# Packed attention and a gated convolution: q, k and p turned on VectorE in 32x32 blocks, scores in 32x32 array tiles, and three smaller moves

## The chip, the core and the metric

The kernel runs on one core of one Trainium2 chip. The core has a matrix engine (TensorE, PE in the profile), VectorE (DVE), ScalarE (ACT), GpSimd (POOL) and SyncE (SP), which issues the kernel's DMAs. Each works through its own queue in order, and they meet at semaphores. Operands lie in SBUF, 128 partitions wide; TensorE writes to PSUM, which TensorE's results leave through VectorE or ScalarE. The metric is the device time of one launch in microseconds. The profile's span is the part of it from the first to the last instruction of the program.

## The reference, cut to what matters

```python
batch, n_heads, seq, head_dim, n_pack = 8, 8, 576, 64, 32

def sm_attn(qq, kk, vv):
    s = scale * np.matmul(qq, kk.transpose(0, 1, 3, 2))     # scale = 1/8
    s = s - np.max(s, axis=-1, keepdims=True)
    a = np.exp(s)
    a = a / (np.sum(a, axis=-1, keepdims=True) + 1e-09)
    return np.matmul(a, vv)

p_packed = sm_attn(p, k, v)                  # 32 packed rows over 576 tokens
x = sm_attn(q, p_packed, p_packed)           # 576 tokens over 32 packed rows
# heads side by side: x is (8, 576, 512)
gate = sigmoid(causal depthwise convolution of x over the tokens, 5 taps, conv_w)
out = (gate * (x @ w_val)) @ w_out
```

All inputs are fp32 except that the three weights arrive as 64-bit floats, which the kernel takes apart itself.

## The kernel before

Eight batches go through the same chain. In `ORDER` a letter names a stage of a batch, the digit the batch, and `.n` repeats it; each token runs a stage's Python generator to its next `yield`. So the string fixes the order of work on every engine's queue by hand (`InOrder` keeps it), and a token that issues on one engine stands in that engine's queue exactly where the string has it. The stages:

- `K`, `Q`, `V`, `P`, `L` are loads on SP's queue: k, q and v in two pieces a batch (`load`, `load_v`), p for one batch twice over (`load_p`), the weights in nine steps (`load_weights`).
- `W`, `C`, `O` make fp32 weights of the 64-bit words (`from_double`): a scaling on ACT, three bit operations and a product on DVE, then sums on POOL or DVE. `w_out` is split in a high and a low part (`woh`, `wol`).
- `k` and `q` turn k and q so that the head dimension lies on the partitions (`transposed`): six groups of six TensorE transposes a batch for each, of 64x64, through a big PSUM tile and out by an ACT copy that also puts tokens in another order (`(a i b)` and `(i a b)`). `k` starts with `turned`, which does the same for p and scales it.
- `a` (`attn_pack`) is the first attention: `scores`, the maximum on DVE, the exponential with its sum on ACT, transposes of the result in pieces of 96 tokens (`at`, three pairs for each half of the heads), copies, the product with v (`pv`) and the division on ACT (`ppd`). `p` (`packed_turned`) turns the packed rows.
- `s` (`attn_out`) is the second softmax: scores, a turn in 32x32 blocks on DVE out of PSUM, the maximum on DVE, the subtraction on POOL, the exponential on ACT. `t` (`weighted`) sums on DVE, divides on POOL, turns back on DVE, and splits the result into `a2h` and `a2l`.
- `w` (`packed_values`) multiplies the packed rows with `w_val`, so that `v` (`value`) is a product with 32 rows for each head; `v` takes three products of split operands on TensorE, the multiplication with the gate on DVE, the high part on ACT (`gvh`), the low part on DVE (`gvl`).
- `x` (`mixed`) makes x and copies it to `xp`, and `g` (`gate`) convolves it: for each of four column blocks one ACT operation for the first tap, four DVE operations for the others, and a tanh on ACT. Batch 0 (`WHOLE`) goes through `convolved` instead: the packed rows are multiplied with the taps on POOL (`kx`) and TensorE accumulates five shifted products into PSUM; ACT's tanh reads them there, and `g` is empty.
- `o` (`project`) multiplies `gvh` and `gvl` with `woh` and `wol`, 12 products of 512 columns for 128 rows, copies the result and stores it (`put`). The tokens of a batch lie in two planes, even and odd ones, since k and q are read in pairs of tokens (`c=2`), so a store goes out in pieces.

`scores` works with 64 rows of the head dimension by 32 packed rows: eight tiles of the array, four heads by two planes. Products of fp32 operands stand as two records each in the profile.

PSUM has three big tiles of two banks each (`big`), one of one bank (`mid`) and one for `o` (`out`). k, q, scores, x, val and wp all take big tiles. SBUF buffers are counted in `NB`: two for each piece of k, q and v, so that loads run about one batch ahead.

The bar `|` in `ORDER` is where the buffers of the weights' words are given up: `gvh` and `gvl` take their place, so the first `gvh` waits for the last weight. Ahead of the bar stand all of `W`, `C` and `O`, and the loads of the first three to four batches.

Of the kernel before, what the change touches and what calls it, by code (L numbers as in the profile page):

```python
# [26 lines left out]
 'p': 2,  # L27
# [78 lines left out]
def packed_attention_gated_conv(  # L106
# [79 lines left out]
    def load_p(b):  # L186
        t = st["p", b] = tile_of("p", [P, G, 2, D], F32, f"p_{b}")
        for twice in range(2):
            sp.dma_start(t[:, :, twice, :], p[b].rearrange("(g x) j d -> (x j) g d", g=G))
        yield  # L190

    def load(b, nm, src):
        for g in range(G):
            m = st[nm, b, g] = tile_of(f"{nm}m", [P, NB9, 2 * D], F32, f"{nm}m_{b}_{g}")
            sp.dma_start(
                m, src[b, 4 * g : 4 * g + 4].rearrange("h (i n c) d -> (h i) n (c d)", n=NB9, c=2)
            )
            yield
# [17 lines left out]
    def words_of(nm, src, rows):  # L216
        words = tile_of("words", [P, DM, 2], U32, f"{nm}_words", stage)[:rows]
        each = rows // len(src)
        for n, s in enumerate(src):
            sp.dma_start(  # L220
                words[n * each : n * each + each].rearrange("a b c -> a (b c)"), s.bitcast(U32)
            )
# [45 lines left out]
    def paired(x):  # L268

        return x.rearrange("a (j g d) -> a g j d", g=G, d=D)  # L270

    def value_weights(b):
        for c in range(NC):
            words = st["words", "wv"][c]
            yield from from_double(f"wv{c}", words, P)
            pool.tensor_tensor(
                paired(wv[:, c, :]),
                st["top", f"wv{c}"].rearrange("a (g j d) -> a g j d", g=G, d=D),
                words[:, :, 0].bitcast(F32).rearrange("a (g j d) -> a g j d", g=G, d=D),
                op=ALU.add,  # L280
            )
            yield

    def conv_weights(b):
# [3 lines left out]
        taps = words[:, :, 1].bitcast(F32)  # L288
        dve.tensor_tensor(
            paired(taps),  # L290
            top.rearrange("a (g j d) -> a g j d", g=G, d=D),
            words[:, :, 0].bitcast(F32).rearrange("a (g j d) -> a g j d", g=G, d=D),
            op=ALU.add,
        )
# [39 lines left out]
    def transposed(b, nm):  # L334

        for g in range(G):
            m = st[nm, b, g]
            xT = st[f"{nm}T", b, g] = tile_of(f"{nm}T", [P, 4, HS], F32, f"{nm}T_{b}_{g}")
            if nm == "k":
                to = xT.rearrange("x (u j) (a i b) -> x u j i b a", u=2, a=NA, i=32)  # L340
            else:
                to = xT.rearrange("x (u j) (i a b) -> x u j i b a", u=2, a=NA, i=32)
            for part in range(NA):
                pt = big(f"{nm}pt_{b}_{g}_{part}")[:, :, : 64 * NA]
                for n in range(NA):
                    for u in range(2):
                        rows = slice(64 * u, 64 * u + 64)
                        pe.transpose(
                            pt[:, u, 64 * n : 64 * n + 64],
                            m[rows, part * NA + n if nm == "q" else n * NA + part, :],  # L350
                            ident[rows, rows],
                        )
                yield
                act.copy(to[:, :, :, :, :, part], pt.rearrange("x u (n j i) -> x u j i n", n=NA, j=2))
# [391 lines left out]
```

## Time and profile before

| | |
|---|---|
| median of three runs | 309.01 us (308.19 to 310.87) |
| the profiled execution | 306.13 us, of which the span is 304.3 us |
| granted TensorE clock in it | 0.994 of full speed |
| read from HBM, written | 33.57 MB, 9.44 MB |
| DMA packets | 22061, of which 6149 under 512 B |

The page gives an engine's busy time as a union: two operations that overlap in its pipeline count once. Its 40 slices show the same busy shares along the span. A row of a group names the engine, the operation, what is written and read, the shape and the count; behind the bar come the busy time in us and the mean of one operation in ns; behind a second bar the idle time before them and what ended most of it. Nearly all lines are L89, that of `InOrder`, so groups are told apart by their tiles. A row of the chain of waits has a start, a length and what ran.

### The profile page before, as it was taken

What the parts mean: (1) busy time and instruction counts of PE and PEld (TensorE: products, weight loads), DVE (VectorE), ACT (ScalarE), POOL (GpSimd) and SP (SyncE); (2) the same over time, 40 slices, a digit from 0 to 9 for tenths busy, and PEclk for the clock granted to TensorE, in tenths of its full rate; (3) what the DMA queues carried; (4) which work ended last, traced back from release to release, by engine and by line L of the source; (5) the groups of instructions that cost most, each with busy time, mean ns of one, the idle gap of its engine ahead of it and who ended that gap; (6) DMA issues with size and microseconds to landing.
All of it is one profiled execution on the core that took longest, in us unless ns stands there. A gap on an engine that the chain in (4) does not pass through costs nothing.

```text
span 304.3 us, 8095 instructions
## 1 busy us (share of the span) xinstructions
PE 278.2 (91%) x3396; PEld 202.0 (66%) x3396; DVE 249.2 (82%) x388; ACT 207.2 (68%) x421; POOL 58.0 (19%) x62
## 2 busy tenths in 40 slices
PE   1677998968999999999999999999999999999993
PEld 0433555546777677667667767877778776878872
DVE  0465478966989999999899989997999899958761
ACT  2554767847987789778967687768758874565421
POOL 1111352241303120241023101310232003400000
PEclk9999999997999999999999999999999999999999
DMA  7999997281866364674442531445471021211105
GB/s 214 315 234 302 266 235 189 56 241 45 254 198 182 116 155 173 185 218 139 123 149 58 170 111 42 148 112 152 155 216 45 2 69 38 69 71 45 58 0 172
DMA packets 22061, 43.52 MB, mean 143 GB/s; under 512 B 6149, under 2 KB 12293, under 8 KB 22026
## 3 DMA queue, kind: packets, MB, share of 16 engines
q1 hardware_dynamic: 22026, 43.02, 49.5%
q8 instruction: 26, 0.43, 0.6%
q14 instruction: 9, 0.07, 0.1%
HBM read 33.57 MB, written 9.44 MB: 141 GB/s over the span
## 4 chain that ended last, share of the span: by engine, by line
PE 53%; DVE 26%; ACT 10%; issue 4%; DMA 2%; POOL 2%; SPq 2%; ACTq 0%; DVEq 0%; POOLq 0%
PE o L89 20%; DVE sig L89 14%; PE val L89 12%; PE x L89 4%; PE s L89 4%; PE pv L89 3%; PE at L89 3%; DMA wv_words<-in_moe_w_val_dram 2%; DVE mx L89 2%; DVE t L89 2%; ACT sig L89 2%; PE qpt L89 2%; PE kpt L89 2%; SPq L89 2%; DVE gvl L89 2%
## 5 line engine op out<-in xcount | busy, mean ns | idle before, releaser
L89 DVE SCALAR_TENSOR_TENSOR sig<-xp,cw,sig 128x576 f32<-128x576 f32 x112 | 97.4, 870 | 6.5 <-ACT sig L89 5.0
L89 PE MATMUL o<-woh,gvh 128*128 128x512 f32 x144 | 58.9, 409 | 0.8 <-ACT osb L89 0.7
L89 PE MATMUL o<-woh,gvl 128*128 128x512 f32 x144 | 56.4, 392 | 0.0
L89 PE MATMUL o<-wol,gvh 128*128 128x512 f32 x144 | 56.3, 391 | 0.0
L89 PE MATMUL val<-a2h,wph 128*128 128x288 f32 x128 | 40.8, 319 | 4.7 <-ACT qT L89 4.5
L89 POOL TENSOR_TENSOR t<-t,mx 128x576 f32<-128x576 f32 x16 | 23.7, 1481 | 87.8 <-DVE mx L89 87.8
L89 PE MATMUL val<-a2h,wpl 128*128 128x288 f32 x128 | 38.4, 300 | 0.0
L89 PE MATMUL val<-a2l,wph 128*128 128x288 f32 x128 | 38.3, 299 | 0.0
L89 POOL TENSOR_TENSOR t<-t,rs 128x576 f32<-128x576 f32 x16 | 20.6, 1288 | 69.3 <-DVE rs L89 34.0
L89 PEld LDWEIGHTS o<-woh,gvh 128*128 128x128 f32 x144 | 27.0, 188 | 9.1 <-ACT osb L89 2.8
L89 ACT ACTIVATE sig<-sig 128x576 f32<-128x576 f32 x28 | 19.3, 688 | 18.4 <-DVE sig L89 18.2
L89 PEld LDWEIGHTS o<-woh,gvl 128*128 128x128 f32 x144 | 27.0, 188 | 6.2
L89 PEld LDWEIGHTS val<-a2h,wph 128*128 128x128 f32 x128 | 24.6, 192 | 9.4 <-ACT qT L89 4.9
L89 DVE TENSOR_TENSOR gvl<-sig,gvh 128x576 fp32r<-128x576 f32 x32 | 25.0, 783 | 6.6 <-ACT gvh L89 6.6
L89 PEld LDWEIGHTS o<-wol,gvh 128*128 128x128 f32 x144 | 27.1, 188 | 4.7
L89 ACT COPY osb<-o 128x512 f32<-128x512 f32 x34 | 20.0, 589 | 14.1 <-PE o L89 13.7
L89 ACT CAST gvh<-sig 128x576 fp32r<-128x576 f32 x32 | 21.6, 676 | 11.5 <-DVE sig L89 7.4
L89 ACT COPY qT<-qpt 128x384 f32<-128x384 f32 x48 | 26.8, 564 | 3.2 <-PE qpt L89 3.1
L89 DVE SCALAR_TENSOR_TENSOR sig<-sig,val 128x576 f32<-128x576 f32 x32 | 23.7, 742 | 5.5 <-ACT sig L89 3.0
L89 ACT COPY kT<-kpt 128x384 f32<-128x384 f32 x48 | 22.5, 482 | 5.6 <-PE kpt L89 5.1
L89 PEld LDWEIGHTS val<-a2h,wpl 128*128 128x128 f32 x128 | 24.7, 193 | 0.2
L89 PEld LDWEIGHTS val<-a2l,wph 128*128 128x128 f32 x128 | 24.7, 193 | 0.0
(82 smaller groups left out, 474.6 us busy)
## 6 DMA issues: line engine op xcount, KB each, us to landing
km<-in_k_dram SPq DMA_DIRECT2D x16, 576.0 KB, 6.7
qm<-in_q_dram SPq DMA_DIRECT2D x16, 576.0 KB, 4.9
vm<-in_v_dram SPq DMA_DIRECT2D x16, 576.0 KB, 6.0
out_dram<-osb SPq DMA_DIRECT2D x24, 256.0 KB, 2.4
wv_words<-in_moe_w_val_dram SPq DMA_DIRECT2D x8, 256.0 KB, 7.7
wo_words<-in_moe_w_out_dram SPq DMA_DIRECT2D x8, 256.0 KB, 11.0
out_dram<-osb SPq DMA_DIRECT2D x8, 192.0 KB, 2.4
p<-in_p_dram SPq DMA_DIRECT2D x16, 64.0 KB, 6.5
```

Source lines behind the costliest of these rows:

```text
L89: made = getattr(self.engine, op)(*args, **kw)
```

## The change

k and q are loaded so that a partition holds nine neighbouring tokens of each of two heads in a piece; the pieces of a partition are 2304 bytes where they were 4608. `transposed` is two DVE turns of 128x1152 in 32x32 blocks for each of k and q, with no TensorE and no ACT work; p is turned on DVE too, after one ACT scaling for two batches. The head dimension then lies in two halves of 32 (`h`), so `scores` runs in tiles of 32 rows by 32 columns, accumulates over `h`, and writes both halves of the heads (two big tiles) in one call. Tokens come back to natural order where the scores are read (`in_turn`): ACT's exponential and DVE's turn read PSUM in steps of 32 elements. The first attention's transposes take 64 rows instead of 128 and go through one big tile and one copy. `ppd` has a third block and `p` a third transpose. Since tokens are in natural order, `gate` reads plain shifts and `put` is a single store.

Batches 0 to 2 are convolved on TensorE instead of batch 0 alone. `gvl` moves from DVE to POOL for all batches, `a2l` for batches 0 to 2, and one product of the weights' conversion moves from DVE to ACT (a scaling) and POOL (`rest_on_pool`). `ORDER` is another string; its bar stands after 197 tokens of 924, where it stood after 263 of 1195.

```diff
-WHOLE = (0,)
+WHOLE = (0, 1, 2)
...
     def load_p(b):
+        t = tile_of("p", [P, 2, 4, D], F32, f"p_{b}")
+        for e in range(G):
+            for c in range(2):
+                rows = (2 * e + c) * NP
+                of_e = p[b : b + 2].rearrange("b (j e) n d -> e n (b j) d", e=G)[e]
+                sp.dma_start(t[rows : rows + NP].rearrange("a b j d -> a (b j) d"), of_e)
...
+        act.mul(t, t, scale)
...
     def load(b, nm, src):
+        for n in range(2):
+            m = tile_of(f"{nm}m", [P, 2, HS // NP * D], F32, f"{nm}m_{b}_{n}")
+            parts.append(m)
+            at = src[b].rearrange("(j e) (i m) d -> e i j (m d)", e=G, i=2 * NP)
+            sp.dma_start(m, at[:, :, 2 * n : 2 * n + 2])
...
-    def from_double(nm, words, rows, by=1.0, rest_on_pool=False):
+    def from_double(nm, words, rows, by=1.0, rest_on_pool=True):
...
     def transposed(b, nm):
+        for n in range(2):
+            xT = tile_of(f"{nm}T", [P, 2, HS // NP, 2, NP], F32, f"{nm}T_{b}_{n}")
+            parts.append(xT)
+            dve.transpose(
+                xT.rearrange("a j m h i -> a (j m h i)"),
+                st[nm, b][n].rearrange("a j x -> a (j x)"),
+            )
+            yield
...
+    def scores(name, of, xT):
+        two = [big(f"{name}_{e}")[:, :, :HS] for e in range(G)]
+        for h in range(2):
+            for j in range(4):
+                for e in range(G):
+                    for c in range(2):
+                        rows = heads[2 * e + c]
+                        pe.matmul(
+                            two[e][heads[j], c, :],
+                            of(rows, j, h),
+                            xT[j // 2][rows, j % 2, :, h, :],
+                            start=(h == 0),
+                            stop=(h == 1),
+                        )
+        return two
+
+    def in_turn(x):
+        return x.rearrange("a c (m i) -> a c i m", i=NP)
...
     def attn_pack(b):
+            a1t = tile_of("a1t", [TP, 2, NB6, 2 * NP], F32, f"a1t_{b}_{g}")
+            at = big(f"at_{b}_{g}")[:TP, :, : 2 * NB6 * NP]
+            at = at.rearrange("x u (n y) -> x u n y", y=2 * NP)
+            for n in range(NB6):
+                for u in range(2):
+                    rows = slice(64 * u, 64 * u + 64)
+                    pe.transpose(
+                        at[:, u, n], a1s[g][rows, n :: NB6], ident[rows, rows]
+                    )
...
     def attn_out(b):
-            dve.transpose(t2[:, g].rearrange("a (c y) z -> a c (y z)", c=2), s2)
+            dve.transpose(
+                t2[:, g].rearrange("a y z -> a (y z)").rearrange("a (c i m) -> a c i m", c=2, i=NP),
+                in_turn(s2s[g]),
+            )
...
     def weighted(b):
-            dve.tensor_tensor(al[:, gs], a2[:, gs], ah[:, gs].bitcast(F32), op=ALU.subtract)
+            (pool if b < 3 else dve).tensor_tensor(al[:, gs], a2[:, gs], ah[:, gs].bitcast(F32), op=ALU.subtract)
...
     def value(b):
-            dve.tensor_tensor(
+            pool.tensor_tensor(
                 lo, gv, hi.bitcast(F32), op=ALU.subtract
             )
...
     def put(osb, row0, c):
+        sp.dma_start(out_f[row0 + c * P : row0 + c * P + P, :], osb)
```

More of the change, by code (lines that the diff above doesn't have):

```diff
@@ L217, in words_of @@
         words = tile_of("words", [P, DM, 2], U32, f"{nm}_words", stage)[:rows]
[L218 to L222, printed above, removed]
+        sp.dma_start(words.rearrange("a b c -> a (b c)"), src.bitcast(U32))
         return words
@@ L276, in value_weights @@
             pool.tensor_tensor(
[L277 to L280, printed above, removed]
+                wv[:, c, :], st["top", f"wv{c}"], words[:, :, 0].bitcast(F32), op=ALU.add
             )
@@ L287, in conv_weights @@
         top = st["top", "cw"]
[L288 to L294 removed]
+        taps = top
+        dve.tensor_tensor(top, top, words[:, :, 0].bitcast(F32), op=ALU.add)
         yield
@@ L334, in transposed @@
     def transposed(b, nm):
[L336 to L351, printed above, removed]
-                        )
-                yield
-                act.copy(to[:, :, :, :, :, part], pt.rearrange("x u (n j i) -> x u j i n", n=NA, j=2))
-                yield
@@ L357, in scores @@
-    def scores(name, pT, xT, g):
-        s2 = big(name)[:, :, :HS]
-        for j in range(4):
-            for c in range(2):
-                rows = slice(D * c, D * c + D)
-                pe.matmul(s2[heads[j], c, :], pT[rows, g, heads[j]], xT[rows, j, :], start=True, stop=True)
-        return s2
-    def turned(b, nm, x, by):
-        pt = one(f"{nm}t_{b}")
-        for g in range(G):
-            pe.transpose(pt[:, g * P : g * P + P], x[:, g].rearrange("a c d -> a (c d)"), ident)
-        yield
-        xT = st[nm, b] = tile_of(nm, [P, G, P], F32, f"{nm}_{b}")
-        act.mul(xT, pt[:, : G * P].rearrange("a (x y) -> a x y", y=P), by)
-        yield
@@ L375, in keys @@
-    def keys(b):
-        yield from turned(b, "pT", st["p", b], scale)
+        parts = st[f"{nm}T", b] = []
+        for n in range(2):
+            xT = tile_of(f"{nm}T", [P, 2, HS // NP, 2, NP], F32, f"{nm}T_{b}_{n}")
[4 more added lines that the diff above has]
+            )
+            yield
+    def scores(name, of, xT):
[11 more added lines that the diff above has]
+                            stop=(h == 1),
+                        )
+        return two
@@ L429, in packed_turned @@
     def packed_turned(b):
-        yield from turned(b, "ppT", st["ppd", b], 1.0)
+        pt = one(f"ppTt_{b}")
+        for n in range(3):
+            pe.transpose(pt[:, n * P : n * P + P], st["ppd", b][:, n], ident)
+        yield
+        ppT = st["ppT", b] = tile_of("ppT", [P, 3, P], F32, f"ppT_{b}")
+        act.copy(ppT, pt[:, : 3 * P].rearrange("a (n x) -> a n x", n=3))
+        yield
     def attn_out(b):
@@ L434, in attn_out @@
         mx = tile_of("mx2", [P, G, NBLK], F32, f"mx2_{b}")
+        s2s = scores(
+            f"s2_{b}", lambda rows, j, h: st["ppT", b][rows, h, heads[j]], st["qT", b]
+        )
+        yield
         for g in range(G):
-            s2 = scores(f"s2_{b}_{g}", st["ppT", b], st["qT", b, g], g)
-            yield
-            dve.transpose(t2[:, g].rearrange("a (c y) z -> a c (y z)", c=2), s2)
+            dve.transpose(
+                t2[:, g].rearrange("a y z -> a (y z)").rearrange("a (c i m) -> a c i m", c=2, i=NP),
+                in_turn(s2s[g]),
+            )
             yield
@@ L489, in packed_values @@
                 rows = slice(D * g, D * g + D)
-                pe.matmul(wp[heads[j], g, :], ppT[rows, g, heads[j]], wv[rows, j, :], start=True, stop=True)
+                pe.matmul(wp[heads[j], g, :], ppT[rows, 2, heads[j]], wv[rows, j, :], start=True, stop=True)
         yield
@@ L524, in mixed @@
             for n in range(2):
-                act.copy(xps[n][:, :, half, PAD:], two[n][:, :, :HS])
+                act.copy(xps[n][:, :, PAD + half * HS : PAD + half * HS + HS], two[n][:, :, :HS])
                 yield
     def convolved(b):
-        kx = tile_of("xp", [P, 2, 2, PAD + HS], F32, f"kx_{b}")
-        kx = kx.rearrange("a n c m -> a (n c m)")[:, : G * NT * D]
+        kx = tile_of("xp", [P, 2, PAD + S], F32, f"kx_{b}")
+        kx = kx.rearrange("a n m -> a (n m)")[:, : G * NT * D]
         kx = kx.rearrange("a (g k d) -> a g k d", g=G, k=NT)
@@ L547, in convolved @@
             for back in range(NT):
-                src = (half + back) % 2
-                skip = (back + src - half) // 2
+                skip = back if half == 0 else 0
+                end = half * HS + HS - back
                 for g in range(G):
```

190 lines of the change are left out of this document (80 added, 110 removed).

## The prediction

> **What bounds the kernel now.** I read the page's engine totals first, then its 40 slices, then the stages.
>
> ```profile
> span 304.3 us, 8095 instructions
> PE 278.2 (91%) x3396; PEld 202.0 (66%) x3396; DVE 249.2 (82%) x388; ACT 207.2 (68%) x421; POOL 58.0 (19%) x62
> PE   1677998968999999999999999999999999999993
> DVE  0465478966989999999899989997999899958761
> DMA  7999997281866364674442531445471021211105
> GB/s 214 315 234 302 266 235 189 56 241 45 254 198 182 116 155 173 185 218 139 123 149 58 170 111 42 148 112 152 155 216 45 2 69 38 69 71 45 58 0 172
> ```
>
> The shares alone make PE and DVE rivals; the slices part them. PE stands at 9 from slice 11 to the end, while DVE is low in the first eight slices and again in the last five. The table by stage (engine busy time, clock, DMA share, GB/s) puts numbers to it. It is cut at 66 us, about where the order's bar lies (stage buffers given up for gvh and gvl), and at 80 and 260:
>
> ```profile
> core 0: us, PE busy (x) PEld busy (x) DVE busy (x) ACT busy (x) POOL busy (x), PEclk, DMA share, GB/s
> 0.00:66.00 66.00, 50.40 (x850) 29.22 (x850) 40.97 (x76) 39.68 (x92) 16.73 (x20) 1.00 0.88 230
> 66.00:80.00 14.00, 10.24 (x160) 8.15 (x158) 8.98 (x16) 9.75 (x21) 5.32 (x6) 0.88 0.51 137
> 80.00:260.00 180.00, 178.26 (x2174) 132.66 (x2174) 170.35 (x259) 138.62 (x279) 33.77 (x34) 1.00 0.44 130
> 260.00:304.00 44.00, 39.35 (x220) 31.99 (x218) 28.88 (x40) 19.17 (x31) 2.22 (x4) 1.00 0.20 69
> ```
>
> Three stages follow. Up to 66 us neither engine is full and the DMA share is 0.88: loads and dependencies set the pace. From 80 to 260 us PE is idle for 1.7 us and DVE for 9.7: PE is the bound, DVE close behind. At the end PE works alone. Behind 66 us PE has 278.2 - 50.4 = 227.8 us of work in 238.3 us, so 10.5 us of idling. The chain's last pieces show the tail:
>
> ```profile
> PE 53%; DVE 26%; ACT 10%; issue 4%; DMA 2%; POOL 2%; SPq 2%; ACTq 0%; DVEq 0%; POOLq 0%
> 294.96 0.76 DVE L89 TENSOR_TENSOR gvl<-sig,gvh 128x576 fp32r<-128x576 f32 x1 [0.74 <-ACT gvh L89]
> 290.85 5.50 PE o L89 x24
> 297.01 3.03 PE o L89 x12
> ```
>
> DVE's last gvl ends at 295.7, the last product at 300.0; the 4.3 us behind it are the copy and the store.
>
> **What goes away, and its price.**
>
> ```profile
> L89 PE MATMUL kpt<-ident,km 64*128 64x64 f32 x288 | 19.6, 260 | 3.2 <-DMA km<-in_k_dram 2.8 <-ACT sig L89 0.2
> L89 PE MATMUL qpt<-ident,qm 64*128 64x64 f32 x288 | 18.8, 246 | 0.3 <-ACT sig L89 0.2
> L89 PE MATMUL pTt<-ident,p 128*128 128x128 f32 x16 | 4.1, 348 | 6.1 <-DMA p<-in_p_dram 6.1
> L89 PE MATMUL at<-ident,a 128*96 128x128 f32 x96 | 21.8, 312 | 2.9 <-ACT a1t L89 2.5 <-ACT pT L89 0.2
> L89 ACT COPY qT<-qpt 128x384 f32<-128x384 f32 x48 | 26.8, 564 | 3.2 <-PE qpt L89 3.1
> L89 ACT COPY kT<-kpt 128x384 f32<-128x384 f32 x48 | 22.5, 482 | 5.6 <-PE kpt L89 5.1
> L89 DVE SCALAR_TENSOR_TENSOR sig<-xp,cw,sig 128x576 f32<-128x576 f32 x112 | 97.4, 870 | 6.5 <-ACT sig L89 5.0
> L89 DVE TENSOR_TENSOR gvl<-sig,gvh 128x576 fp32r<-128x576 f32 x32 | 25.0, 783 | 6.6 <-ACT gvh L89 6.6
> L89 DVE TENSOR_TENSOR a2l<-a,a2h 128x576 fp32r<-128x576 f32 x16 | 12.2, 763 | 1.1 <-ACT a2h L89 1.1
> L89 DVE SCALAR_TENSOR_TENSOR wo_words<-wo_words 128x512 f32<-128x512 uint32 x4 | 2.8, 690 | 0.1
> ```
>
> PE loses the turns of k, q and p: 19.6 + 18.8 + 4.1 = 42.5 us. ACT loses 49.3 us of copies; it was at 207 and is nowhere the bound, so that alone buys nothing. DVE loses the gates of batches 1 and 2, 32 x 0.870 = 27.8; gvl, 25.0; six a2l, 4.6; eight products of the weights' halves, 8 x 0.69 = 5.5. Together 62.9 us.
>
> **What comes in.** The nearest rows:
>
> ```profile
> L89 DVE STREAM_TRANSPOSE a<-t 128x576 f32<-128x576 f32 x16 | 12.3, 768 | 0.1
> L89 DVE TENSOR_TENSOR sm<-sm,eps 128x18 f32<-128x18 f32 x16 | 2.8, 178 | 0.5
> 7.48 1.23 PE L89 MATMUL kpt<-ident,km 64*128 64x64 f32 x18 [0.68 <-DMA km<-in_k_dram]
> 48.92 2.65 PE x L89 x80
> 112.06 0.67 PE x L89 x16
> 75.00 0.65 PE s L89 x16
> 73.85 0.81 PE pv L89 x48
> L89 PE MATMUL ppTt<-ident,ppd 128*128 128x128 f32 x16 | 3.4, 297 | 0.5 <-ACT ppd L89 0.5
> L89 POOL TENSOR_TENSOR wv<-wv_top,wv_words 128x512 f32<-128x512 f32 x4 | 5.1, 1284 | 18.9 <-DVE wv_words L89 18.9
> ```
>
> DVE gets 32 turns of 128x1152. No row has that size. Two of 576 stand for one at most, 1.54 us. The tiny operation of 18 elements takes 0.178 us, so (0.768 - 0.178)/558 is 1.06 ns for each further element, and 1152 come to 1.37 us; were the fixed part 0.3, it would be 1.24. I take 1.37, so 43.8 us (40 to 49). Eight turns of 128x256 for p come to 0.43 each in the same way, 3.4 us. DVE: 249.2 - 62.9 + 43.8 + 3.4 = 233.5, before contention. Its turns and maxima of the scores read PSUM in strides of 32 now; the trace has no such read on DVE, and a few tenths on 32 operations would be up to 10 us, in the range.
>
> PE's new scores: a set was two calls of 16 records on eight array tiles, two records to a tile, 0.65 us a call, 1.3 us a set. Now it is one call of 64 records on sixteen tiles, four records to a tile: twice the 0.65, again 1.3 us. The x rows bear that out: ten records to a tile take 2.65 us, two take 0.67, so 0.25 us for each further one. Change: nothing. By the x rows a set could take 0.67 + 2 x 0.25 = 1.17, -2 us in all; were records issued one by one at the s row's 0.65/16 = 0.04 us, a set would take 2.6 us, +21 us; the pv row (48 records in 0.81 us, 0.017 each) speaks for the low end.
>
> The trace's 0.017 us per record can be set against the Trainium skill, TensorE: Matmul & The Clock Gate, "Wait — 56ns, not 53.3ns?", which says that matmuls never start closer than about 25 ns however small. By that rule a set of 64 would need 1.6 us and the 16 sets 4.8 us more, 291 us for the whole. The pv row disagrees with the floor.
>
> The at turns become 192 of half the rows; 18 of that kind took 1.23 us, 0.068 each, 13.1 us for 21.8 (with strided weights, unknown here, at most the old 21.8). A third ppT turn adds 1.7. Convolving batches 1 and 2 on PE adds four halves of 2.65 - 0.67, 7.9 us. PE: 278.2 - 42.5 - 8.7 + 1.7 + 7.9 = 237 us (235 to 267).
>
> POOL gets 32 gvl and 6 a2l at 1.284 x 576/512 = 1.44 (54.7 us), nine weight products at 1.28 (11.5) and two kx: 58 becomes some 128 of 280. Its queue is in order, so the subtraction and division of the second softmax now stand behind gvl, and ACT's exp and DVE's turn of a2 behind those; one such wait is 1.44 us and is covered as long as DVE has other work, which at 80 to 260 it has. In the tail the last gvl costs 1.44 - 0.78 = +0.7 us on the path.
>
> SP has fewer stores (36 for 48) and the same bytes; p comes for two batches at once in four loads, ahead of the bar twice, and its one buffer holds SP's queue only until the second batch's turn, which stands some fifty tokens ahead of the next load. Loads ahead of the bar come to 15.4 MB in either order, counted from the tokens, which at the 230 GB/s of the first stage is 66 us again. The k and q rows come in pieces half as long, so I see no faster head.
>
> **The sum.** I counted both orders' tokens with these durations. Before: 278.7 us of PE, 42.7 ahead of the bar; the page has 278.2. (For DVE the count is 258 where the page has 249, since its operations overlap a little.) After: 237 of PE, 26 ahead of the bar and 211 behind; DVE has 49 ahead of it, where it had 44. So much of PE's relief lies in the head, where it isn't worth anything, and what counts is the stage behind the bar: 236 becomes 211. The measured head held 7.7 us more PE work than the count (50.4 against 42.7: PE runs ahead of the bar, and lone calls are longer), so 211 - 6 = 205 remain at 66 us. Span: 66 + 205 + 10.5 idle = 282. DVE's own sum: 233.5 + 7 of contention (below) + 25 idle in the head (66 - 41) + 9 behind its last work = 274; it is just below, so PE stays the bound by a little. The profiled execution took 306.1 us for its span of 304.3, and the median is 309.0, 0.9% more: 282 + 1.8 = 284, put to the median 286.
>
> **The rivals.**
>
> ```profile
> L89 DVE SCALAR_TENSOR_TENSOR sig<-xp,cw,sig 128x576 f32<-128x576 f32 x17 | 13.9, 817 | 2.9 <-ACT sig L89 2.5
> 130.79 2.69 DVE L89 SCALAR_TENSOR_TENSOR sig<-xp,cw,sig 128x576 f32<-128x576 f32 x2
> 131.19 1.67 POOL L89 TENSOR_TENSOR t<-t,mx 128x576 f32<-128x576 f32 x1
> L89 DVE SCALAR_TENSOR_TENSOR sig<-sig,val 128x576 f32<-128x576 f32 x32 | 23.7, 742 | 5.5 <-ACT sig L89 3.0
> ```
>
> Slower: GpSimd and VectorE block each other. The first row is the gate in the last 40 us, where POOL does nothing: 0.817 against 0.870 over all. Beside the POOL operation at 131.19, two gates took 2.69 us, 1.05 more than 2 x 0.82. So a POOL operation costs DVE (0.870 - 0.817) x 112 = 5.9 us over the 41 tensor operations of POOL (32 of the second softmax, eight of the weights, kx), 0.14 on average, and 1.05 at worst. The 49 new ones cost 7 to 51 us. I take 7: the average is over operations placed as these are, among mixed DVE work, and turns and reductions, which take one operand, make up more of DVE now. It decides from (304.3 - 34 - 233.5)/49 = 0.75 us each; at 1.05 the span is 233.5 + 51 + 34 = 319, some 324 us as a median. The Trainium skill, SBUF — State Buffer, "Who interferes with whom", says that a DVE instruction with two SBUF inputs and a GpSimd instruction that reads SBUF exclude each other for a whole instruction; the pair at 130.79 agrees with it, and so does the other multiply-add, whose second input is in PSUM and which stays at 0.742.
>
> Little gain: scores now hold two of the three big PSUM tiles until DVE and ACT have read them. If PE stood for a reduction and an exp, 1.5 us, in each of 16 sets, that is 24 us and a span of 306; half of it 294, a median of 298. For it: val also frees its tile only through DVE. Against it: 25 big tiles a batch become 15, and PE went 180 us with 1.7 of idling.
>
> More gain: the head isn't bound by its loads. At the 261 GB/s that its first six slices average the 15.4 MB take 59 us, at 302 only 51, so the bar could lie some 10 us earlier, and the span end near 272, 276 as a median; with DVE's floor of 274 for the span it hardly goes further than 270.
>
> That PE's removed work was hidden anyway is a rival only for the head, and there it is already counted as worth nothing.
>
> **How the numbers follow.** Forecast (PE bound behind the bar, 276 to 296): 0.70. More gain, 276 or less: 0.08. Little gain, 296 to 306: 0.11. Port contention decides, 306 and up to 324: 0.11. The range 270 to 303 leaves out the contention case and a sliver of the others. A measurement of this kernel tells 1% from no change (its three runs span 0.9%), so faster is below 306: 0.82, with a part of the little-gain case at no change, 0.07, and slower 0.11.
>
> **What would show it.** Right: no kpt and qpt rows; PE near 237 busy; DVE near 240, with 32 turns of 1.3 to 1.4 us; the gate's mean below 0.95; PE at 9 from the bar to the end. Wrong: a gate's mean of 1.2 or more with DVE at 270 (contention); s calls of 2 us or more (issue of small tiles); PE idle for tens of us between 80 and 260 us, released by DVE (PSUM tiles); the first gvh well away from 66 us (the head).

## The result, and the profile after

| | before | after |
|---|---|---|
| median | 309.94 us (308.19 to 310.88) | 301.01 us (298.55 to 301.14) |
| ratio, 95% interval | | 0.970 (0.963 to 0.977) |
| the profiled execution's span | 304.3 us | 299.2 us |

The changed kernel is 3.0% faster. The forecast was 286 us, 7.5% less; 301 lies near the upper end of the range of 270 to 303. The first fence is the page of the changed kernel: the span, the engines' totals, and the slices of PE and of its granted clock.

```profile
span 299.2 us, 8542 instructions
PE 259.6 (87%) x3676; PEld 192.0 (64%) x3676; DVE 245.2 (82%) x349; ACT 164.4 (55%) x306; POOL 124.6 (42%) x107
PE   0465555989999998999999999999999979999984
PEclk9998555899999999999999999999999979999998
```

PE's busy time fell by 278.2 - 259.6 = 18.6 us, ACT's by 42.8, DVE's by 4.0, and the span by 5.1. So PE's idle time grew by 13.5, from 26.1 to 39.6. The table by stage says where (busy time of PE, PEld, DVE, ACT and POOL, then clock, DMA share and GB/s, as in the table of before):

```profile
0.00:66.00 66.00, 37.15 (x838) 22.51 (x838) 46.70 (x75) 32.74 (x65) 28.66 (x30) 0.79 0.87 238
66.00:80.00 14.00, 12.95 (x257) 9.82 (x244) 13.55 (x23) 8.47 (x15) 13.92 (x11) 1.00 0.63 183
80.00:260.00 180.00, 175.91 (x2417) 133.10 (x2423) 163.14 (x230) 107.16 (x201) 73.84 (x63) 0.99 0.41 126
260.00:299.20 39.20, 33.63 (x188) 26.54 (x172) 21.80 (x24) 16.05 (x26) 8.14 (x6) 0.98 0.18 68
```

Ahead of 66 us PE does 13.3 us less and the time stays: as forecast, that part buys nothing. The first gvh starts at 68.9 us, where it started at 68.6 (rows of gvh, with the first and the last start):

```profile
L82 ACT CAST gvh<-sig x32: 658/675/687, 68.9 to 288.8; 128x576 fp32r<-128x576 f32 x32
```

Behind 66 us PE is idle for 1.05 + 4.1 + 5.6 = 10.7 us, about the 10.5 forecast, but has 222.5 us of work where 205 were forecast. DVE, whose idle time was 55.1 us of the span before, has 54.0 now: hardly less. The groups of the changed kernel (busy, mean ns, idle before them):

```profile
L82 DVE SCALAR_TENSOR_TENSOR sig<-xp,cw,sig 128x576 f32<-128x576 f32 x80 | 76.5, 957 | 8.7 <-ACT sig L82 7.2
L82 POOL TENSOR_TENSOR gvl<-sig,gvh 128x576 fp32r<-128x576 f32 x32 | 48.4, 1514 | 79.7 <-ACT gvh L82 79.7
L82 DVE STREAM_TRANSPOSE qT<-qm 128x1152 f32<-128x1152 f32 x16 | 21.6, 1358 | 0.0
L82 DVE STREAM_TRANSPOSE kT<-km 128x1152 f32<-128x1152 f32 x16 | 21.5, 1350 | 2.6 <-DMA km<-in_k_dram 2.5
L82 DVE STREAM_TRANSPOSE pT<-p 128x256 f32<-128x256 f32 x8 | 3.4, 429 | 0.9 <-ACT p L82 0.9
L82 PE MATMUL at<-ident,a 64*96 64x64 f32 x192 | 13.4, 281 | 1.8 <-ACT a L82 1.8
```

The turns cost what they were put at, and so do the at turns. The gate does not: 957 ns, where 870 was the mean before and 950 was named as the bound of being right. The chain of waits shows the tail, which PE ended alone before. Now DVE's gates of batch 7 stand on it from 270 us on (some of its pieces: start, length, what ran):

```profile
271.62 2.08 DVE sig L82
273.72 0.83 DVE sig L82
277.67 2.08 DVE sig L82
284.58 1.86 DVE sig L82
```

A gate takes 0.83 us, or 2.08 where GpSimd's subtraction runs beside it, as this row of the timeline has it for the first:

```profile
271.64 1.43 POOL L82 TENSOR_TENSOR gvl<-sig,gvh 128x576 fp32r<-128x576 f32 x1 [8.55 <-ACT gvh L82]
```

### The profile page after: what moved, and what is told of

It reads as the page before. It is cut to its first block, busy times and chain, and to the rows that moved or that the text cites. A ratio compares the mean times of both kernels' runs of the same rounds, so it can differ in the third digit from the quotient of the medians.

```text
span 299.2 us, 8542 instructions
## 1 busy us (share of the span) xinstructions
PE 259.6 (87%) x3676; PEld 192.0 (64%) x3676; DVE 245.2 (82%) x349; ACT 164.4 (55%) x306; POOL 124.6 (42%) x107
## 4 chain that ended last, share of the span: by engine, by line
PE 56%; DVE 23%; DMA 9%; ACT 5%; issue 3%; SPq 2%; POOL 1%; POOLq 1%; ACTq 0%; DVEq 0%
PE o L82 23%; DVE sig L82 13%; PE val L82 11%; PE x L82 8%; PE s L82 5%; DMA vm<-in_v_dram 3%; PE pv L82 3%; DMA wo_words<-in_moe_w_out_dram 3%; PE at L82 3%; DMA km<-in_k_dram 2%; DVE sm L82 2%; DVE kT L82 2%; SPq L82 2%; PE wp L82 1%; ACT sig L82 1%
## 5 line engine op out<-in xcount | busy, mean ns | idle before, releaser
L82 DVE SCALAR_TENSOR_TENSOR sig<-xp,cw,sig 128x576 f32<-128x576 f32 x80 | 76.5, 957 | 8.7 <-ACT sig L82 7.2
L82 POOL TENSOR_TENSOR gvl<-sig,gvh 128x576 fp32r<-128x576 f32 x32 | 48.4, 1514 | 79.7 <-ACT gvh L82 79.7
L82 PE MATMUL o<-woh,gvl 128*128 128x512 f32 x144 | 57.3, 398 | 1.0 <-POOL gvl L82 1.0
L82 PE MATMUL o<-wol,gvh 128*128 128x512 f32 x144 | 56.9, 395 | 0.0
L82 PE MATMUL val<-a2h,wph 128*128 128x288 f32 x128 | 39.6, 310 | 0.0
L82 PE MATMUL val<-a2h,wpl 128*128 128x288 f32 x128 | 37.8, 295 | 0.0
L82 DVE SCALAR_TENSOR_TENSOR sig<-sig,val 128x576 f32<-128x576 f32 x32 | 23.7, 740 | 9.9 <-PE val L82 5.6
L82 POOL TENSOR_TENSOR t<-t,mx 128x576 f32<-128x576 f32 x16 | 20.8, 1299 | 19.5 <-DVE mx L82 19.4
L82 PE MATMUL pv<-vm,a1t 96*32 96x64 f32 x768 | 16.7, 239 | 13.9 <-ACT a1t L82 8.0
L82 PEld LDWEIGHTS pv<-vm,a1t 96*32 96x32 f32 x768 | 13.4, 121 | 22.5 <-ACT a1t L82 14.4
L82 PE MATMUL s<-kT,pT 32*32 32x288 f32 x512 | 17.2, 479 | 12.1 <-DVE kT L82 11.7
L82 ACT CAST gvh<-sig 128x576 fp32r<-128x576 f32 x32 | 21.5, 673 | 10.5 <-DVE sig L82 9.4
```

The lines of the kernel that those rows point to most:

```text
L82: made = getattr(self.engine, op)(*args, **kw)
```

## The experiments

Each ran beside the kernel before on the same chip; a ratio is to that one. Where one leaves work out, its expectation says which.

**Is TensorE the only bound of the kernel before?** Its turns twice (the pair of `pe.transpose` in `transposed`):

```diff
+                        for again in range(2):
                             pe.transpose(pt[:, u, 64 * n : 64 * n + 64], ...)
```

> The kernel before with each TensorE turn of k and q issued twice. It measures what one of the 576 turns costs on the path. PE theory: the 348 behind 79 us add 0.048 us each, 17 us, those ahead of it little: 322 to 332 us against 309. At the price that the prediction used, 0.068 us for all 576, it would be 348. If the turns only fill gaps of PE: 309 to 314.

Measured: 317.79 us, ratio 1.034 (1.027 to 1.041), some 10 us for 576 further records: less than the PE theory's 322, more than the 314 of records that only fill gaps. Without q's turns and copies, and without those of both k and q (a constant tile takes the place of the result):

```diff
+        for g in range(G):
+            st[f"{nm}T", b, g] = any_x
...
+        return
```

> The kernel before without the turns of q: 288 TensorE turns and 48 ScalarE copies are left out, and a constant stands in q's place in the second softmax (q is still loaded). It measures what half of the removed work was worth. The prediction's price, 18.8 us by the group row or 0.068 us each: 290 us or less against 309. Stream theory (behind 79 us q's turns hold PE for 9.9 us, in the head they are worth nothing): 297 to 301. If they only fill gaps: 306 to 309.

> The kernel before without the turns of k and of q: all 576 TensorE turns and their 96 ScalarE copies are left out, and a constant stands for both (k and q are still loaded). It is what taking this work from TensorE can give at best in that order of work. The prediction's terms (38 us of PE, 25 of it behind the bar): 284 us or less against 309. Stream theory, from q alone (ratio 0.980): twice that, 295 to 300.

Measured: 303.67 us, 0.980 (0.973 to 0.988), and 307.06 us, 0.994 (0.988 to 0.999); neither lies in a range that was named for it. The page of the one without either, totals and chain of waits:

```profile
span 304.5 us, 6816 instructions
PE 256.7 (84%) x2820; PEld 181.1 (59%) x2820; DVE 249.3 (82%) x388; ACT 166.8 (55%) x325; POOL 59.2 (19%) x63
DVE 37%; PE 30%; DMA 18%; ACT 6%; issue 4%; POOL 2%; SPq 2%; ACTq 0%; POOLq 0%; DVEq 0%
```

The same kernel in the table by stage:

```profile
80.00:260.00 180.00, 166.50 (x1818) 122.16 (x1810) 169.68 (x257) 114.04 (x219) 33.91 (x34) 0.97 0.40 118
```

21.5 us of PE's busy time and 40 of ACT's are gone, and the span is that of before. From 80 to 260 us PE is 11.8 us less busy and DVE as busy as before (169.68 for 170.35): DVE's 10 us of idling there are no slack that it can give up. Now the other side, DVE relieved and PE not, by leaving gvl out (the third product takes gvh), and both:

```diff
-            dve.tensor_tensor(lo, gv, hi.bitcast(F32), op=ALU.subtract)
...
-        for n, (w, x) in enumerate(((gvh, woh), (gvh, wol), (gvl, woh))):
+        for n, (w, x) in enumerate(((gvh, woh), (gvh, wol), (gvh, woh))):
```

> The kernel before without gvl: VectorE's 32 subtractions (25 us) are left out, and the third product takes gvh in gvl's place, so PE does the same work. Leaving PE's turns out was worth 2 us. One-bound theory for VectorE (PE's relief is worth nothing because VectorE alone sets the pace): 25 us less, 284 to 290. Two-bound theory (PE and VectorE stand at the same height, either one alone holds the time): 300 to 307.

> The kernel before without gvl (as in the other run) and without the TensorE turns and copies of k and q (a constant stands for them). Two-bound theory: both engines are relieved, so more than the two single reliefs together: 280 to 290. If the pace is set by neither but by the chain of waits of a batch: 300 or more.

Measured: without gvl 305.65 us, 0.992 (0.987 to 0.998); without both 299.51 us, 0.968 (0.958 to 0.978). The page's chain of the one without gvl:

```profile
PE 73%; DVE 9%; ACT 7%; DMA 4%; issue 4%; POOL 2%; SPq 0%; ACTq 0%; POOLq 0%; DVEq 0%
```

and in the table by stage:

```profile
80.00:260.00 180.00, 179.45 (x2213) 134.46 (x2209) 156.94 (x240) 141.56 (x284) 34.44 (x35) 1.00 0.46 134
```

Either relief alone is worth under 1%, both together 3.2%. TensorE and VectorE were two bounds of about the same height. With both relieved the two-bound theory had 280 to 290, though; 299.51 is far above that, so something else stands close behind them, and no run here says what. That q's turns alone gave 2%, more than k's and q's together, shows how far a fixed order adds or takes a few us of its own: differences of 1% between such kernels settle nothing.

**What bounds the changed kernel?** The same there: without the third product (gvl is still computed), without DVE's turns of k and q, and without both:

```diff
-        for n, (w, x) in enumerate(((gvh, woh), (gvh, wol), (gvl, woh))):
+        for n, (w, x) in enumerate(((gvh, woh), (gvh, wol))):
```

> The changed kernel without the third product of the projection (gvl with woh: 144 of 432 records, 33 us of PE); gvl itself is still computed. If PE's sum alone sets the pace behind the bar: 268 to 273 us against 301. If VectorE follows close behind (245 us busy, and 34 idle at both ends): 279 to 288. If VectorE and the waits between queues set it: 290 or more.

> The changed kernel without VectorE's 32 turns of k and q (43 us of VectorE; a constant stands for k and q, which are still loaded). If only PE's sum sets the pace behind the bar: 295 to 302 us against 301, the gain being the head's. If VectorE's queue is on the path beside PE's (putting 24 us of gvl back on it and taking 15 us of waiting off cost 8): 285 us or less.

> The changed kernel without VectorE's turns of k and q (43 us of VectorE, a constant stands for them) and without the third product (33 us of PE). Each alone gave 298 and 296 against 301. Two-bound theory: both bounds fall, 265 to 275. If something else (loads, GpSimd, the chain of waits) stands at the same height: 290 or more.

Measured: 296.19 us, 0.954 (0.946 to 0.962); 298.39 us, 0.961 (0.953 to 0.969); 290.33 us, 0.941 (0.932 to 0.950). The changed kernel stands at 0.970, so the reliefs of 22.5 us on PE, of some 43 on DVE, and of both bring about 5, 3 and 9 us. The last was put at 265 to 275 by the two-bound theory and missed that, as its counterpart in the kernel before did. The page of the first, with its chain:

```profile
span 294.8 us, 8250 instructions
PE 237.1 (80%) x3532; PEld 169.6 (58%) x3532; DVE 247.7 (84%) x349; ACT 164.1 (56%) x306; POOL 125.6 (43%) x107
DVE 49%; PE 28%; ACT 8%; DMA 6%; issue 4%; POOL 2%; SPq 1%; DVEq 0%; ACTq 0%; POOLq 0%
```

This kernel has the 237 us of PE that the prediction counted, and ends at 295 with DVE as half of its chain, not at 282. Last, gvl left out, the subtraction on GpSimd with it (the third product takes gvh):

```diff
-            pool.tensor_tensor(lo, gv, hi.bitcast(F32), op=ALU.subtract)
```

> The changed kernel without gvl: GpSimd's 32 subtractions are left out, the third product takes gvh. VectorE is no longer held up by them (the gate's mean of 0.957 us should fall to 0.85, 9 us in all), PE's work is the same. Two-bound theory: 296 to 301, as VectorE's relief by 43 us gave 298. Blocking theory (GpSimd's hold on VectorE is what eats the gain): 290 or less.

Measured: 291.26 us, 0.943 (0.936 to 0.950). Its page, with the chain and the gate's row:

```profile
span 289.9 us, 8511 instructions
PE 256.7 (89%) x3676; PEld 190.9 (66%) x3676; DVE 231.7 (80%) x349; ACT 164.2 (57%) x306; POOL 77.0 (27%) x75
PE 80%; DMA 6%; DVE 4%; issue 3%; ACT 3%; SPq 1%; POOL 1%; DVEq 0%; ACTq 0%; POOLq 0%
L82 DVE SCALAR_TENSOR_TENSOR sig<-xp,cw,sig 128x576 f32<-128x576 f32 x80 | 66.1, 826 | 10.2 <-ACT sig L82 8.9
```

The same kernel in the table by stage:

```profile
0.00:66.00 66.00, 38.43 (x848) 23.21 (x850) 46.88 (x76) 32.86 (x65) 29.72 (x30) 1.00 0.87 238
80.00:260.00 180.00, 179.83 (x2467) 136.23 (x2466) 156.10 (x231) 110.55 (x206) 37.68 (x38) 1.00 0.42 128
```

32 subtractions on another engine are gone, TensorE's work is the same, and the span falls by 9.3 us. TensorE is busy for 179.83 of 180 us and is 80% of the chain: 290 is its own bound in this order. DVE lost 245.2 - 231.7 = 13.5 us without having lost an instruction, 10.4 of it on the gates.

Both kernels issue their products in the same order (the third with gvh in gvl's place), so their traces can be laid side by side: TensorE in the changed kernel is 1.4 us behind the other at 78 us, 4.3 at 229, 7.8 at 247 and 9.3 at the end. The largest step stands in the changed kernel's chain, and behind it the same twelve products without gvl:

```profile
234.83 1.50 DVE sig L82 x2
236.35 2.08 DVE sig L82
238.46 1.61 DVE sig L82
241.53 0.58 ACT osb L82
242.16 4.61 PE o L82 x12
```

```profile
235.96 3.06 PE o L82 x12
```

Two gates take 2.08 and 1.61 us for 0.83, ScalarE's tanh waits for the last gate, the copy of osb stands behind that tanh in ScalarE's queue, and TensorE waits 2.1 us for the copy. Its granted clock is then 0.57 from 242.2 to 246.2 us, and twelve products take 4.61 us. So VectorE's delay reaches TensorE through ScalarE's queue; for gvl itself TensorE waits only 1.0 us in all, by its row of o<-woh,gvl.

**Is it GpSimd's hold on VectorE?** The hold is the time by which a VectorE operation is longer because one of GpSimd runs beside it. The subtraction twice, the second time into a tile that is read no more:

```diff
             pool.tensor_tensor(lo, gv, hi.bitcast(F32), op=ALU.subtract)
+            pool.tensor_tensor(gv, gv, hi.bitcast(F32), op=ALU.subtract)
```

> The changed kernel with each gvl subtraction on GpSimd issued twice, the second into a tile that nobody reads any more, so that gvl itself is no later than before and only GpSimd's traffic doubles. Theory that this traffic holds VectorE back and that this is the 10 us between the changed kernel and the one without gvl: 308 to 312 us, and a mean gate above 1050 ns (957 with one, 826 with none). If the 10 us are the waits of TensorE for gvl and not VectorE's hold: 301 to 304 us, gate below 1000 ns.

Measured: 319.31 us, 1.041 (1.031 to 1.050). Page, chain and gate:

```profile
span 316.1 us, 8567 instructions
PE 266.3 (84%) x3676; PEld 194.5 (62%) x3676; DVE 259.0 (82%) x349; ACT 164.6 (52%) x306; POOL 178.4 (56%) x139
DVE 41%; PE 29%; POOL 12%; ACT 6%; DMA 5%; issue 4%; SPq 1%; DVEq 0%; ACTq 0%; POOLq 0%
L82 DVE SCALAR_TENSOR_TENSOR sig<-xp,cw,sig 128x576 f32<-128x576 f32 x80 | 87.5, 1094 | 9.6 <-ACT sig L82 8.4
```

With 0, 32 and 64 subtractions on GpSimd DVE is busy for 231.7, 245.2 and 259.0 us: 0.42 and 0.43 us for each. The gate takes 826, 957 and 1094 ns; 2, 12 and 24 of the 80 gates take more than 1.2 us. That is the blocking theory's result for the gate; the span grew by 16.9 us, more than its 7 to 11. GpSimd itself is 12% of this chain, where it was 1% of the changed kernel's: the next gvl can stand behind the added operation in its queue, and this run doesn't separate that part from the hold. The Trainium skill, SBUF — State Buffer, "Who interferes with whom", has a VectorE instruction with two SBUF inputs contend for a shared port pair with a GpSimd instruction that reads SBUF; the 2.08 us gates and this row of three agree. Moving the subtraction alone, back to DVE in the changed kernel and to GpSimd in the kernel before:

```diff
-            pool.tensor_tensor(
+            dve.tensor_tensor(
                 lo, gv, hi.bitcast(F32), op=ALU.subtract
```

> The changed kernel with gvl back on VectorE, all else kept. PE theory (behind the bar PE is the bound in both kernels; the change took little PE work away there, because the turns of k and q cost only some 0.048 us each when they run in a stream, and convolving two more batches and 1.6 us for a score set ate most of that): PE's work is the same, so 296 to 304 us against 301. VectorE's busy time goes from 245 to about 254 (32 x 0.75 = 24 us come in, some 15 us of waiting for GpSimd go). Blocking theory (PE only looks busy, GpSimd's gvl holds VectorE's gate operations up, and that sets the pace): 290 us or less.

> The kernel before with gvl on GpSimd instead of VectorE, nothing else. PE theory: VectorE's sum falls by about 25 - 15 us, PE's stays, so 305 to 310. If VectorE's queue is on the path as much as PE's (putting gvl back cost the changed kernel 8 us): 299 to 304. If GpSimd's holding up of gate operations weighs more where there are 112 of them: 312 or more.

Measured: 308.72 us, 1.001 (0.996 to 1.005), and 321.74 us (315.97 to 323.32) against 311.33, whose runs scatter too much for a ratio. The first lies outside what both theories had, 296 to 304 and 290 or less. So in the new order the place on GpSimd is worth 8 us in spite of the hold (DVE is at 257.8 busy with gvl, 245.2 without it), and in the old order it costs 5 by its fastest run and 10 by its median. Each order was written for its own placement; a single move out of it is no clean measure.

**What do the small scores cost?** All of `scores` twice, and a second pass over a third of the columns:

```diff
+        for again in range(2):
             for h in range(2):
...
-                            two[e][heads[j], c, :],
+                            two[e][heads[j], c, : HS // (1 + 2 * again)],
```

> The changed kernel with the products of every score set issued twice (the second pass starts anew, the result is the same). PE theory: 16 sets x 1.55 us = 25 us more PE work, of which the four sets in the head count little: 318 to 327 us. Blocking theory: PE has room, so 301 to 309 us.

> The changed kernel with a second pass over every score set on only 96 of the 288 columns (the same values are written again). The full second pass cost 25.5 us, 0.025 us for each of 1024 records. If a record of the 32x32 tiles costs its issue, whatever its length: the third costs as much, 322 to 328 us. If it costs its columns: 8 to 9 us, so 309 to 311.

Measured: 326.49 us, 1.061 (1.053 to 1.068), and 318.69 us, 1.028 (1.020 to 1.037). The first fence has two sets in the changed kernel's chain, one in the head and one behind the bar; the others have a set in the chain of the kernel with two passes and of the one with a pass and a third:

```profile
30.31 2.51 PE s L82 x63
97.59 1.53 PE s L82 x63
```

```profile
112.94 2.90 PE s L82 x125
```

```profile
108.18 2.26 PE s L82 x85
```

Taken from the first to the last record, a set takes 1.60 us, 2.97 twice, and 2.33 with the third: 1.37 for a full pass of 64 records and 0.73 for a short one. So a full set costs more than the 1.3 us forecast, but the ten sets behind 79 us occupy 16.6 us in the changed kernel, 3.6 more than at 1.3 each, and not twice as much, as single issue would have it. In the times, 16 further passes cost 25 to 28 us, more than their 22, and 16 short ones 18, more than their 12; the 318.69 lies between what was put for a price by issue and by columns.

**Which batches belong on TensorE?** Batch 1 convolved on it in the kernel before; batch 7 too in the changed one; batch 7 in place of batch 2 there; and a product of `ident` that nobody reads issued before every second token ahead of the bar, to keep TensorE's clock up in the head:

```diff
-WHOLE = (0,)
+WHOLE = (0, 1)
...
-WHOLE = (0, 1, 2)
+WHOLE = (0, 1, 2, 7)
...
-WHOLE = (0, 1, 2)
+WHOLE = (0, 1, 7)
...
+            if fill and at % fill == fill - 1:
+                pe.matmul(idle[:, :P], ident, ident, start=True, stop=True)
```

> The kernel before with batch 1 convolved on PE as well (its gate tokens dropped, the rest of x's tokens of batch 1 set behind the last of v's of batch 0). PE gets 2 x 2.4 = 4.8 us, VectorE loses 16 gate operations, 13 to 14 us. PE theory: 311 to 315. If VectorE's relief counts for as much as PE's burden: 304 to 309.

> The changed kernel with batch 7 convolved on PE as well (its gate stage is empty), order otherwise the same. PE gets 2 x 2.4 = 4.8 us more, VectorE loses 16 gate operations, which from 264 us on stand in the chain at 6.05 us for each of the four column blocks. PE theory in its strict form (only PE's sum counts): 303 to 306 us. Tail theory (the last 25 us of the changed kernel are a chain of gate operations that GpSimd's gvl holds up, 2.08 us for 0.83): 290 to 297 us.

> The changed kernel with batches 0, 1 and 7 convolved on TensorE in place of 0, 1 and 2: batch 2 goes through the gate on VectorE, batch 7 doesn't, so VectorE has as many gates as before and TensorE as many products, but 13 us of gate work lie between 80 and 140 us, where VectorE is busy for 15 to 17 of each 20 us, and no longer near the end. Theory that two bounds of about the same height hold the span, VectorE's (with GpSimd's hold) late and TensorE's (290) all through: 295 to 298 us. If TensorE alone sets the end, no gain: 300 to 302. If the order by hand fits only its own placement: 301 to 306.

> The changed kernel with a fill-in product of 128x128 (its result is read by nobody) behind every second entry of the order ahead of the bar. PE's granted clock is at half in the records from 27.6 to 54.9 us, and score sets there take 2.6 us for 1.53. If the cold clock in the head is on the path: 293 to 298 us against 301. If the head is set by loads and VectorE: 300 to 302. If the fill-ins stand in the way of the chain of the first batches: 304 or more.

Measured: 313.87 us, 1.014 (1.006 to 1.022); 304.13 us, 0.989 (0.982 to 0.996); 318.07 us, 1.034 (1.028 to 1.040); and 309.79 us against 308.88, from four runs of which one took 301.55, two 309.8 and one 1387 us, so that no ratio is given and the clock's part stays open. None beats the changed kernel. Batch 7 on TensorE came out where the strict PE theory had it, at 303 to 306. The third was to take 13 us of gates from the tail; its stages from 120 to 140 and from 280 us on:

```profile
120.00:140.00 20.00, 11.03 (x116) 7.22 (x116) 16.38 (x24) 10.64 (x21) 1.16 (x1) 0.75 0.21 60
280.00:318.00 38.00, 32.96 (x231) 26.83 (x230) 4.40 (x6) 7.84 (x16) 5.71 (x4) 1.00 0.17 63
```

The longest of PE's waits about there (what waited for what: us, times, longest):

```profile
PE at L85 <- DVE sig L85: 4.4, 1, 4.4
PE x L85 <- ACT a L85: 3.7, 2, 3.0
```

DVE is indeed done early, with 4.4 us of work in the last 38, but PE idles for 9 us from 120 to 140, half of it behind a gate, and ends alone and late. It missed by 20 us what it was put at, and says only that the order must move with the work; whether gates placed earlier can pay stays open.

## Why the prediction came out as it did

**Right.** The direction; the head (first gvh at 68.9 us, 66 forecast, and TensorE's 13.3 us of relief ahead of it worth nothing); the turns (1.35 for 1.37 us, 0.43 for 0.43); the at turns (13.4 for 13.1 us); POOL's sum (124.6 for 128); the little-gain rival set aside, since PE is idle for 4 us from 80 to 260 and not for tens.

**The step that failed first: DVE's floor.** The prediction had DVE's "own sum: 233.5 + 7 of contention (below) + 25 idle in the head (66 - 41) + 9 behind its last work = 274". The idle time in it was too small. It was 55 us in the profile before, and the step kept 34 of it, as if the 21 us between were PE's doing and would go with PE's load. Most of them stay when PE is relieved: 55.2 without the turns (304.5 - 249.3), 54.0 in the changed kernel, 47.1 where PE has 237 us of work. The waits of DVE in the kernel before, from 80 us on (us, times, longest), name ACT first, not PE:

```profile
DVE sig L89 <- ACT sig L89: 8.1, 8, 2.5
DVE gvl L89 <- ACT gvh L89: 3.6, 5, 0.7
```

With 47 to 55 of idling the floor comes to 233.5 + 7 + 47 to 55 = 288 to 296 before any other error: above the 282 given as PE's bound. So the step "PE stays the bound by a little" fails, and the run with 237 us of PE, which ends at 294.8, shows it. Such a floor is no law: without gvl DVE idles for 58.2 us, because there PE sets the pace.

**The hold.** "a POOL operation costs DVE ... 0.14 on average": 32 gvl alone cost 13.5 us, 0.42 each, where 7 were put for all 49. This is the rival of port contention, right in its mechanism, at a price between its ends (0.14 and 1.05) and short of the 0.75 from which it would have made the kernel slower. That gvl meets gates, with their two operands in SBUF, more often than the second softmax's operations did would explain it; no run separates that. Without gvl the span is 9.3 us shorter: more than half of the 17.2 between the span of 299.2 and the 282 forecast. Taking some 43 us of turns off VectorE brought only 3 us, so these 9 aren't VectorE's sum; the traces point to where the held gates stand, ahead of osb at 242 us and in the tail.

**TensorE's sum.** "205 remain at 66 us" were 218.3 in the kernel without gvl, where PE is busy nearly throughout (256.7 less the 38.43 ahead of 66 us), and that one ended at 289.9. These 13.3 us more of work, less 5 us of idling that went (10.5 forecast, 5.6 there), are the other 8 us of the miss. PE's work behind 66 us fell by 227.8 - 218.3 = 9.5 us, where 227.8 - 205 = 22.8 were counted. Taken from the start of a block of products to that of the next, behind 79 us, and that kernel set against the one before: k's and q's turns had occupied 16.8 us for 348 records, 0.048 each, where 0.068 came from a lone group and would make 23.7; the at turns gave back 1 us, where 8.7 were counted for the whole kernel from rows whose records overlap their neighbours'; x took 8.4 us more (7.9 forecast for all four halves); ten score sets took 15.3 us, 2.3 more than at 1.3 each.

The two together: TensorE's own bound is 290, not 282, and gvl on GpSimd adds 9 to it, of which TensorE's waits for gvl itself are 1.0. Of 278.2 - 237 = 41 us taken from PE on paper, 18.6 came out of its busy time, 13.5 of these became idle time (13.3 of it ahead of 66 us), and 5.1 came off the span.

What stays open: the kernel without turns and third product is relieved by 26 us on PE and 37 on DVE, and still takes 290. Neither engine's sum explains that. Its page names the gates of VectorE first in the chain, with 28% of the span, and gvl still stands beside them on GpSimd; the order's waits on each other may do the rest, but no run separates them.

## What to carry to other kernels

A busy share of 99% makes an engine a bound, not the only one: give every near-full engine a floor of its busy time plus its idle time, and take idle time out of the floor only where the row of what ended it names the engine that is relieved (here 47 to 55 of VectorE's 55 us stayed when TensorE was relieved). Work moved to GpSimd is paid on VectorE by what runs beside it, so price it beside the operations that it will meet, here two-operand gates at 0.42 us per subtraction, and look for the queue that stands behind those. And when an order by hand is part of a change, single edits out of it measure the order as much as the edit.

## What the runs showed of the hardware

- A 128x576 subtraction on GpSimd slows VectorE by 0.42 us on average here, the same for the first 32 and for the next 32.
- A score record on a 32x32 tile costs 0.73/64 = 0.011 us with a third of its columns, and 1.37/64 = 0.021 with all 288. The Trainium skill, TensorE: Matmul & The Clock Gate, "Wait — 56ns, not 53.3ns?", puts a floor of about 25 ns under the start of one product after another; these records go below it, and the first sixteen records of the set at 97.59 us start 6 or 7 ns apart. So the 1.5 us of a set aren't that floor.
- 576 further turns of 64x64 raised the busy time of their two rows from 19.6 + 18.8 = 38.4 us to 28.9 + 28.3 = 57.2, 0.033 each, half of what a lone group shows.
- A score set at 30 us took 2.51 us, where it takes 1.53 behind the bar; the granted clock from 30 to 33 us is 0.50. The kernel without gvl has a granted clock of 1.00 there, and its chain has

```profile
30.41 2.50 PE s L82 x63
```

so that reading doesn't tell how slowly the sparse products of the head run. At 242 us, in a dense stream, it does: twelve products took 4.61 us at 0.57 and 3.06 at 1.00.
